# Recording every operation of an attention and mixture-of-experts kernel and issuing it in the order of a list schedule

## The chip, the core and the metric

The kernel runs on one core of a Trainium2 chip. The core has TensorE (PE, matrix products into PSUM; PEld is its weight load), VectorE (DVE), ScalarE (ACT), GpSimd (POOL) and SyncE (SP, which here issues the DMAs). Each engine works through its own queue in the order in which the program was written out, and an instruction at the head of a queue waits for semaphores of other engines. The metric is the device time of one launch in microseconds; lower is better.

## The reference

Linear attention, then a mixture of eight experts with a Sinkhorn-normalised gate, then a gated feed-forward layer, on 2304 tokens of 512 features:

```python
q_s = softmax(q, axis=-1); k_s = softmax(k, axis=2)          # 4 x 8 heads, 576 x 64
kv = einsum('bhsd,bhse->bhde', k_s, v)
x = einsum('bhsd,bhde->bhse', q_s, kv)                       # -> (2304, 512)
P = exp(x @ w_gate - max)                                    # then 8 rounds of
                                                             # row and column normalisation
for e in range(8):                                           # w1: 512 x 1024, w2: 1024 x 512
    out += P[:, e:e+1] * (maximum(x @ w1[e], 0) @ w2[e])
h = out @ w_in                                               # 512 x 2048
return (h * clip(h + 3, 0, 6) / 6) @ w_out                   # 2048 x 512
```

## The kernel before

Every float32 operand of a large product is split into a float16 head and a float16 rest (`split`, lines 230 to 232, and the `hi`/`lo` pairs), and three or four float16 products stand for one float32 product. Products are further formed as seven block products instead of eight, which needs sums of blocks before and after.

The 16 halves of the experts and the 4 quarters of the feed-forward layer are 20 slices, s = 0 to 19. For each slice the tokens pass in three pairs of 384-token groups, p = 0, 1, 2; one (s, p) is a step. In a step TensorE makes the up products of (s, p) while it makes the down products of the step before. Slices 3 to 13 are the FAST stage, 33 steps of `fast_step`, where the down products use seven block products too: the list `line` in that function writes out by hand the order of the units `u0` to `u6` (up) and the parts of `three(t)` (down, one token tile of 128 at a time, three tiles in a step). All seven PSUM banks of that stage have fixed roles (`place`): X, Y, Z for the up products, N0, N1, T and G for the down products. A tile's down products go through bank G in a chain: ScalarE copies N into G (line 1318), TensorE adds products, ScalarE copies one half of G to the other (line 1325), TensorE adds again, and VectorE adds the finished bank onto `acc` (`onto`, line 1310). Only then may the next tile's line 1318 write G.

Beside this run queues of small steps: `ticks`, `side` (the weights of the next slice: load into the one buffer `raw`, absolute maximum, line 261, sums on GpSimd, line 297, and splits, lines 231 and 232) and `back` (conversion of the float64 feed-forward weights, lines 349 to 380). `tick()` takes one or a few of these steps after each unit. So VectorE, ScalarE, GpSimd and SyncE get their instructions in the order in which the hand-written line, the queues and the calls of `tick` interleave; in two middle stretches the framework's own scheduler orders them. In a FAST step VectorE also makes the sums S1 to S4 (`s_sums`, lines 970 to 976) and once a slice T1 to T4.

SBUF tiles for results of the up products come from pools with 16 (`h`) and 5 (`r`) buffers; PSUM tiles come from pools that are closed and opened again at the borders of the FAST stage.

At the start `attention(0)` handles the first two of four batches, then its products feed slice 0, while `attention(1)` (the second two batches) is put beside slices 0 and 1.

## Time and profile before

| what | value |
|---|---|
| median of 2 runs | 1988.99 us (1985.55 to 1992.42) |
| the profiled execution | 1992.86 us, span 1991.1 us |
| granted TensorE clock over the span | 0.977 of full speed |
| TensorE busy | 1843.3 us (93%) |
| VectorE busy | 1423.8 us (72%) |
| ScalarE, GpSimd busy | 990.0 us, 621.2 us |

The span runs from the first to the last instruction of the core. A clock of 1.00 is 2.4 GHz and 0.50 is 1.2 GHz; a mean between them says what part of the stretch was at either. Busy time of TensorE includes matmuls that ran at the lower clock, so it is more than the time that the same work takes at the full one.

### The profile page before, as it was taken

The page shows a single profiled execution, that of the slowest core. Times are in us where ns is not written, and L with a number is a line of the kernel's source. Part 1 is how long each engine was busy: PE and PEld are TensorE (multiplying, and loading weights), DVE is VectorE, ACT ScalarE, POOL GpSimd, SP SyncE. Part 2 cuts the span into 40 slices and gives each one's busy share as a digit, 9 for nine tenths or more (in the row PEclk, how much of TensorE's full clock was granted, in tenths as well). Part 3 has the DMA queues.
Part 4 walks back from the last instruction along what each step waited for, and adds up shares of the span by engine and source line. Part 5 has one row for each costly group of instructions (what it writes and reads, how often), then busy time and mean ns, then how long its engine had stood idle before and what let it go on. Part 6 is the DMA issues. An engine that isn't in the chain of part 4 may idle for free.

```text
span 1991.1 us, 31140 instructions
## 1 busy us (share of the span) xinstructions
PE 1843.3 (93%) x12183; PEld 1135.5 (57%) x12183; DVE 1423.8 (72%) x2438; ACT 990.0 (50%) x2047; POOL 621.2 (31%) x581
## 2 busy tenths in 40 slices
PE   5989999898989898989898989898989999999999
PEld 3455555465666565656566656575745555455554
DVE  8882866778787888787788777857544777687554
ACT  4646454454545455555445555454533556554342
POOL 3323243333332333333333333222222333233111
PEclk8989999999999999999899999999999999999999
DMA  6700022312131212221212222202020000110001
GB/s 206 217 6 1 22 91 103 120 55 93 54 109 54 93 54 93 69 83 64 93 54 93 69 80 74 97 9 91 1 98 1 22 22 1 43 43 22 1 22 74
DMA packets 62611, 129.29 MB, mean 65 GB/s; under 512 B 13952, under 2 KB 18048, under 8 KB 61952
## 3 DMA queue, kind: packets, MB, share of 16 engines
q1 hardware_dynamic: 62464, 127.30, 18.9%
q8 instruction: 95, 1.56, 0.3%
q14 instruction: 52, 0.43, 0.1%
HBM read 105.92 MB, written 18.61 MB: 63 GB/s over the span
## 4 chain that ended last, share of the span: by engine, by line
PE 59%; DVE 24%; ACT 9%; issue 4%; DMA 2%; POOL 1%; SPq 0%; DVEq 0%; POOLq 0%; ACTq 0%
PE y L1118 15%; PE xplace L1173 8%; PE gplace L1289 4%; PE X L1016 4%; PE yplace L1173 4%; DVE w1buf L232 3%; PE gplace L1297 3%; DVE acc L1310 3%; PE tplace L1297 3%; PE tplace L1289 3%; PE Y L1016 2%; ACT w1buf L231 2%; PE B L1016 2%; PE zplace L1173 2%; PE C L1016 2%
## 5 line engine op out<-in xcount | busy, mean ns | idle before, releaser
L1118 PE MATMUL y<-w2buf,h 128*128 128x512 f16 x1944 | 447.8, 379 | 0.5 <-POOL h L1048 0.4
L1191 POOL TENSOR_TENSOR h<-r,h 128x384 f16<-128x384 f32 x198 | 188.9, 954 | 673.7 <-ACT h L1182 637.2
L1173 PEld LDWEIGHTS <-w1buf 128*128 128x128 f16 x2772 | 275.5, 99 | 170.5 <-issue 26.9
L1016 PEld LDWEIGHTS <-w1buf 128*128 128x128 f16 x2268 | 220.4, 98 | 175.0 <-issue 21.0
L1173 PE MATMUL xplace<-xbuf,w1buf 128*128 128x384 f16 x1584 | 308.3, 332 | 6.5 <-ACT r L1194 2.0
L1118 PEld LDWEIGHTS <-h 128*128 128x128 f16 x1944 | 189.1, 98 | 211.1 <-issue 3.3
L1289 PEld LDWEIGHTS <-xbuf 128*128 128x128 f16 x1584 | 155.8, 99 | 152.1 <-issue 77.6
L1048 POOL TENSOR_TENSOR h<-r,h 128x384 f16<-128x384 f32 x90 | 87.3, 970 | 286.7 <-ACT h L1047 255.9
L1173 PE MATMUL yplace<-xbuf,w1buf 128*128 128x384 f16 x792 | 157.4, 337 | 1.3 <-DVE r L1197 1.1
L1182 ACT ACTIVATE h<-r 128x384 f16<-128x384 f32 x264 | 138.0, 523 | 30.4 <-DVE r L1197 24.1
L1194 ACT ACTIVATE r<-xplace 128x384 f32<-128x384 f32 x198 | 96.4, 487 | 106.3 <-PE xplace L1173 103.8
L1043 POOL TENSOR_TENSOR h<-g,h 128x384 f16<-128x384 f32 x72 | 66.8, 928 | 251.5 <-ACT h L1042 220.2
L1016 PE MATMUL X<-xbuf,w1buf 128*128 128x384 f16 x720 | 139.6, 327 | 3.5 <-ACT r L1029 2.7
L1297 PEld LDWEIGHTS <-h 128*128 128x128 f16 x1188 | 118.2, 99 | 36.6 <-issue 0.3
L1289 PEld LDWEIGHTS <-h 128*128 128x128 f16 x1188 | 117.6, 100 | 29.0 <-issue 2.5
L1197 DVE SCALAR_TENSOR_TENSOR r<-yplace,r 128x384 f32<-128x384 f32 x132 | 73.2, 554 | 80.5 <-ACT r L1194 52.7
L1297 PE MATMUL tplace<-w2buf,h 128*128 128x256 f16 x792 | 122.3, 278 | 0.0
L1029 ACT ACTIVATE r<-X 128x384 f32<-128x384 f32 x120 | 58.2, 487 | 126.1 <-PE X L1016 125.8
L1310 DVE SCALAR_TENSOR_TENSOR acc<-gplace,cf,acc 128x512 f32<-128x512 f32 x99 | 74.0, 748 | 45.2 <-PE gplace L1297 42.1
L1289 PE MATMUL gplace<-kvs,xbuf 128*128 128x256 f16 x396 | 62.5, 276 | 44.1 <-ACT gplace L1318 28.3
L1297 PE MATMUL gplace<-w2buf,h 128*128 128x512 f16 x396 | 102.0, 380 | 0.0
L1042 ACT CAST h<-g 128x384 f16<-128x384 f32 x96 | 48.9, 511 | 94.4 <-DVE g L1041 94.4
(670 smaller groups left out, 3308.1 us busy)
## 6 DMA issues: line engine op xcount, KB each, us to landing
raw<-in_moe_w_dram SPq DMA_DIRECT2D x31, 1024.0 KB, 6.0
xbuf<-xkeep SPq DMA_DIRECT2D x77, 384.0 KB, 6.9
scr<-in_moe_w_in_dram SPq DMA_DIRECT2D x16, 512.0 KB, 4.4
scr<-in_moe_w_out_dram SPq DMA_DIRECT2D x16, 512.0 KB, 3.6
xkeep<-xbuf SPq DMA_DIRECT2D x2, 2688.0 KB, 11.0
out_dram<-acc SPq DMA_DIRECT2D x18, 256.0 KB, 2.0
win<-scr SPq DMA_DIRECT2D x16, 256.0 KB, 2.6
wout<-scr SPq DMA_DIRECT2D x16, 256.0 KB, 2.1
```

The lines of the kernel that those rows point to most:

```text
L1016: nc.tensor.matmul(bank[b], w[:, i, wi, c, fs], x[:, i, xi, c, :], start=(first and n == 0), stop=(last and n == 5), skip_group_check=True,)
L1043: eng.tensor_sub(h[:, 1, :], r, h[:, 0, :])
L1048: eng.tensor_sub(h[:, 1, :], c, h[:, 0, :])
L1118: nc.tensor.matmul(ps, hs[grp][fc][:, hi, ts_], w[:, wi, fc, :], start=(n == 0), stop=(n == 11))
L1173: nc.tensor.matmul(o, w[:, i, wi, c, fs], x[:, i, xi, c, :], start=(first and n == 0), stop=(last and n == 5), skip_group_check=True,)
L1182: nc.scalar.activation(h[:, 0, :], c, AF.Relu if relu else AF.Copy)
L1191: nc.gpsimd.tensor_sub(h[:, 1, :], c, h[:, 0, :])
L1194: nc.scalar.activation(r, b, fn, scale=H_DOWN)
L1197: nc.vector.scalar_tensor_tensor(out=r, in0=b, scalar=H_DOWN, in1=r, op0=ALU.mult, op1=ALU.add)
L1289: nc.tensor.matmul(o, a(qf)[:, hl, ts_], b(qf, 1 - hl), start=(first and n == 0), stop=(n == 3), skip_group_check=True,)
L1297: nc.tensor.matmul(o, hs[grp][fc][:, 0, ts_], w[:, 0, fc, cols], start=False, stop=(fc == 3), skip_group_check=True)
L1310: nc.vector.scalar_tensor_tensor(out=a, in0=ps, scalar=factor(s, p, j), in1=a, op0=ALU.mult, op1=ALU.add)
```

## The change

The name `nc` now stands for a `Planner`, which takes down each operation (engine, name, arguments) instead of issuing it. For each it works out a duration (`cost`) and its dependences: by overlap of byte ranges in SBUF and DRAM (`region`, `meet`, `touch`), and by bank in PSUM, where all operations on a bank stay in the order of the code. Matmuls into one place are joined to operations of at most six. `at` is the sum of TensorE's durations up to the place where the operation was taken down.

`order` then makes a list schedule for the five engines. A deadline `late` is passed backwards from the operations that depend on each other, from `at` for TensorE and `at` plus 60 us for the others. Each engine takes, of what can start first (within 30 ns), the operation with the earliest deadline, may leave itself idle for up to 600 ns for one that is more urgent, and starts nothing more than 40 us ahead of `at`. VectorE operations with two wide SBUF operands, or from SBUF to SBUF without a reduction, and all of GpSimd's exclude each other (`lock`). A DMA takes 60 ns of SyncE and lands after 2500 ns plus its bytes over 150 bytes per ns, whatever else is under way. At the end `issue` writes the operations out in that order. `Planner.add` and `issue` replace the framework's scheduling everywhere; the code that takes operations down (`line`, `tick`, the queues) stays as it was, and so do the operations themselves, their shapes and their engines. All rows of the changed program therefore have line 313.

Pools become fixed places: `ring` gives buffers in turn out of one SBUF tile (16 of `h`, 6 of `r`; the feed-forward's `g` tiles get three places of their own), `bank_of` gives one of eight PSUM tiles that exist throughout.

```diff
+class Planner:
...
+    LEAD = 40000.0
+    SLACK = 60000.0
+    HOP = 120.0
+    MARGIN = 300.0
...
+    def cost(self, eng, name, out, ins):
...
+        if eng == "tensor":
+            four = 4 if ins[0].dtype == F32 else 1
+            return 2.0 + n * 0.4167 * four
+        if eng == "scalar":
+            return 170 + 0.8 * n if psum else (720 if n == 512 else 180 + 0.9 * n)
+        big = max([n] + [self.width(x) for x in ins])
+        if eng == "vector":
...
+            if not psum and (half or not two) and name not in ("tensor_reduce", "reduce_max", "reciprocal"):
+                return 150 + big / 1.92
+            return 150 + big / 0.96 + (60 if big >= 512 else 0)
+        if eng == "gpsimd":
+            if big == 512 and len(out.shape) > 2:
+                return 1610
+            return 70 + (2.25 if len(ins) > 1 else 1.2) * big
+        return 2000.0
...
+    def hop(self, a, b):
+        if a["eng"] == b["eng"] and a["eng"] != "sync":
+            return 0.0
+        if a["eng"] == "tensor":
+            return 170.0 + self.HOP
+        if a["eng"] == "sync":
+            return 2500.0 + a["dma"] / 150.0
+        return self.HOP + (self.MARGIN if b["eng"] == "tensor" else 0.0)
+
+    def order(self):
...
+        for o in reversed(ops):
+            late = o["at"] + (0.0 if o["eng"] == "tensor" else self.SLACK)
+            for b in o["post"]:
+                late = min(late, b["late"] - o["dur"] - self.hop(o, b))
+            o["late"] = late
...
+        def pick(e):
+            f = free[e]
+            c = []
+            for o in waits[e]:
+                s = max(f, ready[o["n"]], o["at"] + lag - self.LEAD)
+                if o["lock"]:
+                    s = max(s, lock["gpsimd" if e == "vector" else "vector"])
+                c.append((s, o["late"], o["n"], o))
+            if not c:
+                return None
+            s0 = min(x[0] for x in c)
+            s, d, _, o = min((x for x in c if x[0] <= s0 + 30), key=lambda x: (x[1], x[2]))
+            if e not in ("tensor", "sync"):
+                end = s + o["dur"]
+                for x in sorted((x for x in c if x[0] < end and x[1] < d), key=lambda x: x[1]):
+                    if x[1] + lag < end and d + lag > x[0] + x[3]["dur"] and x[0] - s < 600:
+                        return x[0], x[3]
+            return s, o
...
+            end = s + o["dur"] * (1.0 if e == "tensor" else 1.05)
+            if e == "sync":
+                free[e] = s + 60.0
+                end = s
...
+    def issue(self):
+        for o in self.order():
+            for f, a, k in o["calls"]:
+                f(*a, **k)
...
-    nc = tc.nc
+    real = tc.nc
+    nc = Planner(real)
...
-    pools(u=1, d=2, m=2)
+    pspool = ctx.enter_context(tc.tile_pool(name="ps", bufs=1, space=bass.MemoryType.PSUM))
+    psum = [pspool.tile([P, 512], F32, tag=f"b{i}", name=f"b{i}") for i in range(8)]
+    which = {"A": [0], "B": [1], "C": [2], "D": [3], "d": [4, 5], "m": [6, 7]}
...
+    def ring(tag, shape, dt, bufs):
+        if tag not in rings:
+            rings[tag] = [cpool.tile([P, bufs] + list(shape[1:]), dt, name=f"ring_{tag}"), 0]
+        r = rings[tag]
+        r[1] += 1
+        return r[0][:, (r[1] - 1) % bufs]
...
-        pools(place=1, m=1)
-        for n in ("x", "y", "z", "n0", "n1", "t", "g"):
-            place[n] = banks["place"].tile([P, 512], F32, tag=n, name=f"{n}place")
+        which["m"] = [7]
+        for i, n in enumerate(("x", "y", "z", "n0", "n1", "t", "g")):
+            place[n] = psum[i]
...
+    with tc.manual_schedule():
+        nc.issue()
```

Three places show how rows move. First VectorE's queue before, in slice 8, where the first weights of slice 9 are split (`w1buf` rows, line 232) beside the sums of the up products (lines 972 and 976); `acc` from `gplace` and `tplace` are the rows that set free bank G and bank T.

```order
L1310 SCALAR_TENSOR_TENSOR acc<-n1place,cf_7762,acc 128x512
L972 TENSOR_TENSOR xbuf<-xbuf,h_0_2_8473 128x768
L232 SCALAR_TENSOR_TENSOR w1buf_86<-raw,ws_a__8496,w1buf_86 128x512
L232 SCALAR_TENSOR_TENSOR w1buf_86<-wtmp,ws_a__8496,w1buf_86 128x512
L976 TENSOR_TENSOR xbuf<-h_0_0_8532,xbuf 128x768
L232 SCALAR_TENSOR_TENSOR w1buf_86<-raw,ws_a__8496,w1buf_86 128x512
L1310 SCALAR_TENSOR_TENSOR acc<-gplace,cf_7762,acc 128x512
L1310 SCALAR_TENSOR_TENSOR acc<-tplace,cf_7762,acc 128x512
L232 SCALAR_TENSOR_TENSOR w1buf_86<-raw,ws_a__8496,w1buf_86 128x512
```

The same splits in VectorE's queue of the changed program, one whole token tile (`b6_67` is bank G, `b5_66` bank T, `b3_64` and `b4_65` the N banks, `b1_62` bank Y, `scr_84` the conversion, `xbuf_77` the sums).

```order
L313 SCALAR_TENSOR_TENSOR acc_85<-b6_67,ring_cf_114,acc_85 128x512
L313 SCALAR_TENSOR_TENSOR acc_85<-b5_66,ring_cf_114,acc_85 128x512
L313 TENSOR_TENSOR xbuf_77<-ring_h_105 128x768
L313 TENSOR_TENSOR xbuf_77<-xbuf_77,ring_h_105 128x768
L313 TENSOR_TENSOR xbuf_77<-ring_h_105 128x768
L313 SCALAR_TENSOR_TENSOR w1buf1_79<-raw_82,ring_ws_108,w1buf1_79 128x512 x4
L313 SCALAR_TENSOR_TENSOR acc_85<-b3_64,ring_cf_114,acc_85 128x512
L313 SCALAR_TENSOR_TENSOR scr_84<-scr_84 128x512
L313 TENSOR_TENSOR xbuf_77<-ring_h_105,xbuf_77 128x768
L313 SCALAR_TENSOR_TENSOR ring_r_104<-b1_62,ring_r_104 128x384
L313 SCALAR_TENSOR_TENSOR scr_84<-scr_84 128x512
L313 SCALAR_TENSOR_TENSOR ring_h_105<-ring_r_104,ring_h_105 128x384
```

The four splits that stood on both sides of the `acc` rows of banks G and T now stand behind them, in front of the row of an N bank; two more rows of 128x512 and 128x384 follow in the changed tile before the next row that frees bank G.

SyncE's queue before, from the weights of slice 0 on (`raw` is its first, `acc<-in_moe_w` its second weight, `xbuf<-in_k` and `xbuf<-in_v` the second pair of batches):

```order
L291 DMA raw<-in_moe_w_dram 128x4x512
L1462 DMA wg<-in_moe_w_gate_dram 128x4x8
L458 DMA acc<-in_q_dram 128x192 x14
L327 DMA acc<-in_moe_w_dram 128x4x512
L458 DMA acc<-in_q_dram 128x384 x2
L1588 DMA xkeep_101<-xbuf 128x5376
```

The same place in the changed program:

```order
L313 DMA raw<-in_moe_w_dram 128x4x512
L313 DMA wg<-in_moe_w_gate_dram 128x4x8
L313 DMA xbuf<-in_v_dram 128x9x64 x2
L313 DMA xbuf<-in_k_dram 128x2x576
L313 DMA xbuf<-in_v_dram 128x9x64
L313 DMA xbuf<-in_k_dram 128x2x576
L313 DMA xbuf<-in_v_dram 128x9x64 x3
L313 DMA acc<-in_moe_w_dram 128x4x512
```

Six of the second batches' `v` loads and two of their `k` loads now stand in front of the second weights of slice 0; the fourteen `q` loads that stood there have moved behind.

## Rows read from the trace of the kernel before

**Rows 1.** The page: span, and busy time of TensorE.

```profile
span 1991.1 us, 31140 instructions
PE 1843.3 (93%) x12183; PEld 1135.5 (57%) x12183; DVE 1423.8 (72%) x2438; ACT 990.0 (50%) x2047; POOL 621.2 (31%) x581
```

**Rows 2.** Busy time in five stretches: length, engines, then clock, DMA share, GB/s.

```profile
0.00:54.00 54.00, 31.93 (x449) 20.76 (x449) 44.16 (x78) 26.16 (x44) 18.04 (x24) 0.87 0.57 190
54.00:106.00 52.00, 42.78 (x238) 21.46 (x238) 43.05 (x55) 33.83 (x58) 16.25 (x14) 0.96 0.70 208
106.00:387.60 281.60, 271.08 (x1941) 148.44 (x1940) 182.94 (x367) 135.58 (x267) 105.00 (x105) 0.98 0.15 50
387.60:1449.90 1062.30, 971.37 (x6756) 668.67 (x6755) 809.65 (x1334) 542.99 (x1207) 342.48 (x302) 0.97 0.21 72
1449.90:1937.00 487.10, 475.75 (x2556) 251.46 (x2554) 318.53 (x565) 236.88 (x447) 131.38 (x129) 0.99 0.08 28
```

**Rows 3.** Waits of TensorE from 387.6 to 1449.9 us: total us, times, longest.

```profile
PE gplace L1289 <- ACT gplace L1325: 35.7, 25, 2.0
PE gplace L1289 <- ACT gplace L1318: 28.3, 15, 2.5
PE gplace L1289 <- DVE xbuf L972: 15.7, 9, 2.8
```

**Rows 4.** Timeline of TensorE: start, length, what, idle before it.

```profile
812.79 0.60 PE L1289 MATMUL gplace<-kvs,xbuf 128*128 128x256 f16 x4
...
841.12 0.78 PE L1289 MATMUL gplace<-kvs,xbuf 128*128 128x256 f16 x4
...
855.36 1.03 PE L1297 MATMUL gplace<-w2buf,h 128*128 128x512 f16 x4
...
861.69 0.60 PE L1289 MATMUL gplace<-kvs,xbuf 128*128 128x256 f16 x4 [2.47 <-ACT gplace L1318]
```

**Rows 5.** Timeline of VectorE behind the wait at 861.69 us.

```profile
858.25 1.61 DVE L976 TENSOR_TENSOR xbuf<-h,xbuf 128x768 f16<-128x768 f16 x1
859.79 0.74 DVE L232 SCALAR_TENSOR_TENSOR w1buf<-raw,ws_a__8496,w1buf 128x512 f16<-128x512 f32 x1
860.45 0.74 DVE L1310 SCALAR_TENSOR_TENSOR acc<-gplace,cf,acc 128x512 f32<-128x512 f32 x1
```

**Rows 6.** Groups of 387.6 to 1449.9 us with shapes: busy us, mean ns, idle before.

```profile
L1197 DVE SCALAR_TENSOR_TENSOR r<-yplace,r 128x384 f32<-128x384 f32 x132 | 73.2, 554 | 80.5 <-ACT r L1194 52.7 <-PE yplace L1173 27.6
L970 DVE TENSOR_TENSOR xbuf<-h,h 128x768 f16<-128x768 f16 x64 | 55.9, 874 | 0.0
```

**Rows 7.** One line's instructions there: shortest, median and longest in ns.

```profile
L970 DVE TENSOR_TENSOR xbuf<-h,h x64: 544/553/1626, 407.6 to 1420.5; 128x768 f16<-128x768 f16 x64
```

**Rows 8.** Timeline of SyncE's issues, start and length.

```profile
21.35 8.42 SPq L458 DMA_DIRECT2D acc<-in_q_dram  x14
33.08 0.38 SPq L327 DMA_DIRECT2D acc<-in_moe_w_dram  x1
...
61.20 18.12 SPq L478 DMA_DIRECT2D xbuf<-in_v_dram  x8
```

**Rows 9.** Timeline of VectorE near the start.

```profile
39.07 1.02 DVE L685 TENSOR_TENSOR xbuf<-f,xbuf 128x384 f16<-128x384 f32 x2 [1.30 <-ACT xbuf L684]
...
48.07 2.33 DVE L261 TENSOR_REDUCE am_b__539<-acc 128x1 f32<-128x1024 f32 x2
...
97.34 4.14 DVE L605 TENSOR_TENSOR acc<-acc,qm 128x1536 f32<-128x1536 f32 x2
101.40 2.33 DVE L261 TENSOR_REDUCE am_b__871<-raw 128x1 f32<-128x1024 f32 x2
```

**Rows 10.** Timeline of TensorE behind those reductions.

```profile
105.51 0.29 PE L208 MATMUL cm_b__894<-identb,wm_b__880 128*128 128x128 bf16 x1 [7.10 <-DVE wm_b__880 L269]
```

**Rows 11.** DMA issues of the page: count, KB each, median us to landing.

```profile
xbuf<-xkeep SPq DMA_DIRECT2D x77, 384.0 KB, 6.9
...
acc<-in_moe_w_dram SPq DMA_DIRECT2D x1, 1024.0 KB, 5.4
```

More of the change, by code (lines that the diff above doesn't have):

```diff
@@ L108, in view, with bank_of @@
         return ap.rearrange(f"p ({dims}) -> p {dims}", **{f"x{j}": shape[j] for j in range(1, len(shape))})
-    def col(name, w=1, dt=F32):
-        return sm.tile([P, w], dt, tag=f"c{w}{dt}", name=name, bufs=8)
+    rings = {}
+    def ring(tag, shape, dt, bufs):
[4 more added lines that the diff above has]
+        return r[0][:, (r[1] - 1) % bufs]
+    def col(name, w=1, dt=F32):
+        return ring(f"c{w}" + ("i" if dt == I32 else ""), [P, w], dt, 8)
+    def bank_of(tag, shape):
+        b = which[tag]
+        b.append(b.pop(0))
+        flat = psum[b[-1]]
+        n = 1
+        for d in shape[1:]:
+            n *= d
+        if len(shape) == 2:
+            return flat[:, :n]
+        dims = " ".join(f"x{j}" for j in range(1, len(shape)))
+        return flat[:, :n].rearrange(f"p ({dims}) -> p {dims}", **{f"x{j}": shape[j] for j in range(1, len(shape))})
     def psm(shape, name, dt=F32):
-        return banks["m"].tile(shape, dt, tag="m", name=name)
+        return bank_of("m", shape)
     def rt(name):
-        return rpool.tile([P, GN], F32, tag="r", name=name)
+        return ring("r", [P, GN], F32, 6)
     ident = cpool.tile([P, P], F32, name="ident")
@@ L271, in fin @@
         def fin():
-            st["s"] = sm.tile([P, 2], F32, tag="ws", name=f"ws_{name}", bufs=8)
+            st["s"] = ring("ws", [P, 2], F32, 8)
             pow2(st["mm"], st["s"], top)
@@ L422, in tile_attention_moe_ffn @@
     AW, VW = H * QR * D, H * QR * (D + 1)
-    half = lambda t: t.rearrange("p j d -> p (j d)")
     GA = QR - GJ
@@ L517, in kback @@
             if first:
-                ps = banks["d"].tile([P, len(cs) * P], F32, tag="d", name=f"kb{b0}_{cs[0]}")
+                ps = bank_of("d", [P, len(cs) * P])
             else:
@@ L547, in kv @@
                 t["kv"] = [
-                    banks["u"].tile([P, 512], F32, tag="AB"[i], name=f"kv{b0 + i}")[:, : NKC * (D + 1)]
+                    bank_of("AB"[i], [P, 512])[:, : NKC * (D + 1)]
                     .rearrange("p (c d) -> p c d", d=D + 1)
@@ L596, in qmax @@
             if "qm" not in t:
-                t["qm"] = sm.tile([P, H, QR], F32, tag="qm", name=f"qm{pr}", bufs=2)
+                t["qm"] = ring("qm", [P, H, QR], F32, 2)
             nc.vector.tensor_reduce(
@@ L916, in factors @@
         r = res[s]
-        ws = sm.tile([P, 1], F32, tag="wsc", name=f"wsc{s}", bufs=3)
+        ws = ring("wsc", [P, 1], F32, 3)
         nc.vector.tensor_mul(ws, r["s1"][:, 1:2], r["s2"][:, 1:2])
@@ L934, in factor @@
         if p not in cf:
-            co = sm.tile([P, 1], F32, tag="co", name=f"co{s}_{p}", bufs=3)
+            co = ring("co", [P, 1], F32, 3)
             nc.vector.tensor_scalar(
@@ L1008, in up_burst @@
             tags = {"X": "AD"[bursts[0] % 2], "Y": "B", "Z": "C"}
-        bank = {b: banks["u"].tile([P, 512], F32, tag=g, name=f"{b}{nm}")[:, :GN] for b, g in tags.items()}
+        bank = {b: bank_of(g, [P, 512])[:, :GN] for b, g in tags.items()}
         fs = slice(qf * P, (qf + 1) * P)
@@ L1112, in down_tile @@
         j = g * GJ + t
-        ps = banks["d"].tile([P, DM], F32, tag="d", name=f"y{s}_{j}")
+        ps = bank_of("d", [P, DM])
         ts_ = slice(t * P, (t + 1) * P)
@@ L1179, in hi @@
         def hi(c, grp, fc, relu):
-            h = hpool.tile([P, 2, GN], F16, tag="h", name=f"h{grp}{s}_{p}_{fc}", bufs=HB)
+            h = ring("h", [P, 2, GN], F16, HB)
             hs[grp][fc] = h
@@ L1441, in x2_steps @@
         return steps
-    with tc.manual_schedule():
-        make_identity(nc, ident)
+    if True:
+        make_identity(real, ident)
         nc.vector.memset(ones, 1.0)
@@ L1511, in bank @@
             if qd == QB22:
-                return banks["u"].tile([P, 512], F32, tag="AB"[i], name=name)[:, :GN]
+                return bank_of("AB"[i], [P, 512])[:, :GN]
             count[0] += 1
             if (count[0] - 1) % 4 < 2:
-                return banks["u"].tile([P, 512], F32, tag="CD"[i], name=name)[:, :GN]
-            return banks["d"].tile([P, DM], F32, tag="d", name=name)[:, :GN]
+                return bank_of("CD"[i], [P, 512])[:, :GN]
+            return bank_of("d", [P, DM])[:, :GN]
         f = t0["forms"](0, bank)
@@ L1652, in tile_attention_moe_ffn @@
     first, last = order.index((FAST[0], turns[FAST[0]][1])), order.index((FAST[-1] + 1, 0))
-    with tc.manual_schedule():
+    if True:
         for sp in order[FROM:first]:
@@ L1664, in tile_attention_moe_ffn @@
             unit(lambda: None)
-        pools(u=1, d=2, m=2)
+        which["m"] = [6, 7]
         for sp in order[last + 1 : TO]:
@@ L1669, in tile_attention_moe_ffn @@
         prev = step(*sp, prev)
-    with tc.manual_schedule():
+    if True:
         for sp in order[AGAIN:]:
```

223 lines of the change are left out of this document (202 added, 21 removed).

## The prediction

> **What bounds the kernel now.** I read the page first. TensorE is busy for 1843.3 us of 1991.1, so at first sight 148 us are to be had [rows 1]. Then I cut the span into stretches, since a mean share over stages with different limits says little [rows 2]. Each stretch gives two losses of TensorE: its length less its busy time, and the clock below 1.00. The start (0 to 106 us) loses 31 us of idle time; the stretch to 387.6 us loses 10.5; the FAST stage, 387.6 to 1449.9 us, loses 91; the stretch behind it 11.4. The FAST stage also runs at a mean clock of 0.97.
>
> What the FAST stage could take is read from a clean step. From one tile's first product into bank G at 812.79 us to the same place one step later, at 841.12 us, is 28.3 us, and in between TensorE hardly pauses [rows 4]. The stage has 33 such steps: 935 us. It takes 1062.3 us. So 127 us lie above its own clean pace, 91 of them idle and the rest work at 1.2 GHz behind the pauses. This is the stage on which the forecast rests.
>
> Who ends TensorE's pauses there: the copy by ScalarE from one half of bank G to the other (35.7 us) and its copy from N into G (28.3 us), then VectorE's sums (15.7 us) [rows 3]. But ScalarE is not the cause. At 861.69 us TensorE had waited 2.47 us for line 1318; the down products into G had been issued from 855.36 us with a length of 1.03 us, so `acc` could have been taken from G at about 856.4 us [rows 4]. VectorE took it at 860.45 us, some 4 us late. In front of it in the queue stood a sum of 1.61 us and weight splits of 0.74 us each, none of them urgent [rows 5]. The queue order of VectorE is what TensorE waits for.
>
> The sum of 1.61 us is itself a wait: the line it is like (970) has a median of 553 ns, a shortest of 544 and a longest of 1626 [rows 7]; 64 of them have a mean of 874 ns [rows 6]. So each lost some 0.3 us on the mean.
>
> **The change, part by part.** All sums are made against the profiled execution, 1992.86 us, which is 3.9 us above the median of the two runs.
>
> (1) The FAST stage. No operation is added or taken away; VectorE, ScalarE and GpSimd get another order, and TensorE small shifts. The diff's order shows the kind of move: before, three splits and a sum stood between an N row and the rows that free G and T; now four splits stand behind those rows, in front of an N row, and an N bank has a twin. Cover for such a tile: TensorE has 28.3 / 3 = 9.4 us of work in it. VectorE's rows in the changed tile are nine of 128x512 at 0.74 us [rows 5], four sums at 0.553 us [rows 7], three of 128x384 at 0.554 us [rows 6] and one short one on the conversion, put at 0.55 us: 6.7 + 2.2 + 1.7 + 0.55 = 11.1 us. So VectorE is 1.6 us over in that tile, and the pauses won't all go. I count such an overrun once for each of the two weights of 11 slices: 22 times 1.6 us, 35 us that stay. Over the whole stage there is room: VectorE's 809.65 us [rows 2] stand against 935 us.
> The bounds: if all overruns are worked off in the neighbouring tiles, 127 us go; if half of the loss stays, 64. I take 127 - 35 = 92 us, because the tile's own rows give the 35.
>
> (2) The middle (106 to 387.6) and the late stretch (1449.9 to 1937) lose 10.5 and 11.4 us of idle time. There is no clean step to compare with; between nothing and 22 us I take half, 11 us.
>
> (3) The start. One part gains. At 105.51 us TensorE had waited 7.1 us for the scale of slice 1's second weights [rows 10]; its absolute maximum ran on VectorE at 101.40 us, behind 4.14 us of subtractions and other work for the second pair of batches [rows 9]. In the changed order this maximum stands ahead of those. If it goes, 7 us are won; what is late next is the split of the same weights, which is needed either way.
> One part may lose. The second weights of slice 0 were issued at 33.08 us, behind fourteen loads of `q` (8.42 us of queue) [rows 8]; they land 5.4 us later [rows 11], at 38.5 us, and VectorE looked at them only at 48.07 us [rows 9]. Now six loads of `v` and two of `k` stand ahead of them. Eight such `v` loads took 18.12 us of queue [rows 8]; six take 13.6 us, and the two of `k` (576 KB each, put at the same pace per KB) some 9 us. They can't start before the first products have freed their places, which is the work of the first 20 to 27 us, so the weights are issued somewhere between 33 and 46 us and land between 38.5 and 51 us. In VectorE's queue the maximum of these weights stands ahead of most rows that make slice 0's inputs, the first of which ran at 39.07 us [rows 9]. The price is therefore between 0 and 12 us, all of it on the path, since TensorE has nothing else yet. I take 2 us, near the lower end, because the issue at 33.08 us was itself behind a wait for the places of `q` that doesn't change, and because the early loads take later waits away. Net for the start: -5 us, with ends at -7 (all of the gain) and +12 (all of the price, and no gain).
> The Trainium skill, page "DMA: Bandwidth & Descriptors", section "Issuing engines are not separate DMA queues", says that all DMAs of a core run on the same 16 engines and interleave. The planner prices each DMA as if it were alone, at which price part (3) would cost nothing; by the page's rule it costs up to the whole 12 us. The trace sides with the page: with 0.70 of the DMA engines busy the core moved 208 GB/s [rows 2].
>
> (4) Fixed rings and banks. They give the same number of `h` buffers, one more of `r`, the same banks. I cost them at nothing: the dependences by place that the pools gave are the same ones by bytes. If a bank were shared where it was not before, one tile would wait for another, which is rival C.
>
> Sum: 1992.9 - 92 - 11 - 5 = 1885 us; less the 3.9 us by which the profiled execution stands above the median, 1881 us.
>
> **The rivals.**
> A, the forecast: pauses of the FAST stage fall to a third, 1880 us.
> B, VectorE becomes the bound: its 809.65 us in the stage hold some of the waiting that [rows 6, 7] show, but little of it goes, the fixed order drifts against the real times, and overruns add up; half of the 127 us stays. 1992.9 - 64 - 5 - 3.9 = 1920 us. For it: 11.1 us of rows in a tile of 9.4. Against: whole steps at 28.3 us exist already.
> C, the change doesn't do what it says: the list is made with prices that don't hold, queues stand behind other rows than before, and what is won at one bank is lost at another. 1985 us, give or take 20. Against: the prices agree with rows here, for instance 150 + 384 / 0.96 = 550 ns against a mean of 554, and 150 + 512 / 0.96 + 60 = 743 ns against 740 [rows 5, 6].
> D, slower: DMAs come late in every slice. Each slice of the FAST stage reloads a set of tokens from `xkeep` in seven DMAs of 384 KB, 77 in all [rows 11]. The planner has each land after 2.5 + 2.6 = 5.1 us; sharing 208 GB/s [rows 2], the seven take 12.9 us, and one weight load that slips between them adds 1024 KB or 5 us: 13 us late. Eleven times that is 143 us of TensorE's time, and 1880 + 143 = 2023 us before the clock, some 2040 with it. It decides from (1989 - 1880) / 11 = 10 us a slice on. Against: the same DMAs stand a whole step (28.3 us) ahead of their use, the planner may start them up to 40 us ahead, and no wait for them is among TensorE's [rows 3].
> By the section of the Trainium skill's page "DMA: Bandwidth & Descriptors" named above, D would be the outcome if the loads had no lead; the trace bears the shared rate out, not the lateness.
>
> **How the numbers follow.** A 0.62, B 0.20, C 0.11, D 0.07. The forecast is A, 1880 us. Its own ends: all parts at their best, 1992.9 - 127 - 22 - 7 - 3.9 = 1833 us; FAST at half with the start at its worst, 1992.9 - 64 + 12 - 3.9 = 1937 us. The range leaves out C and D and the outer edge of A's best case: 1840 to 1937 us. Two per cent of 1989 us is 40 us, about what a measurement of this kernel can tell from no change. Faster by more than that (under 1949 us) are A and B, 0.82; within it most of C, 0.10; slower D and a little of C, 0.08.
>
> **What would show it.** In the changed profile: the FAST stage takes 960 to 980 us at a clock of 0.99 or 1.00 (right), or over 1000 (B). The waits of TensorE for the copies into G fall from 64 us to under 25. The rows of `acc` from bank G start within a microsecond of the products' end. The mean of the sums comes down towards 553 ns if GpSimd and VectorE are really kept apart. The wait of 7.1 us near 105 us is gone; a new wait between 39 and 51 us shows part (3)'s price. D would show as TensorE waiting for a DMA into `xbuf` once a slice. The forecast is wrong if TensorE's pauses keep their sum and only change their names, or if the start grows by more than 12 us.

## The result and the profile after

| what | before | after |
|---|---|---|
| median of 2 runs each | 1988.99 us | 1841.88 us (1840.94 to 1842.81) |
| ratio, 95% interval | | 0.926, 0.919 to 0.933 |
| the profiled execution, its span | 1992.86, 1991.1 us | 1842.81, 1841.0 us |
| granted TensorE clock over the span | 0.977 | 0.989 |

The changed kernel is 147 us faster, and 38 us faster than the forecast of 1880 us. It lies 1.9 us above the lower end of the range, 1840 us. The page of the changed kernel, against [rows 1]:

```profile
span 1841.0 us, 30821 instructions
...
PE 1794.4 (97%) x12183; PEld 1128.1 (61%) x12183; DVE 1374.5 (75%) x2438; ACT 984.3 (53%) x2047; POOL 600.6 (33%) x581
```

Of the 150 us by which the span shrank, TensorE's busy time gives 49 and its idle time 101. The same stretches as in [rows 2], cut where the same operations stand now (FAST begins at 384.62 us and ends at 1317.38 us); the columns are as there:

```profile
0.00:54.00 54.00, 27.05 (x375) 18.03 (x376) 36.18 (x57) 18.86 (x28) 18.51 (x23) 0.79 0.81 251
54.00:106.00 52.00, 46.63 (x535) 27.05 (x536) 48.07 (x73) 34.89 (x62) 15.29 (x12) 0.93 0.31 91
106.00:384.62 278.62, 271.73 (x1713) 147.36 (x1712) 179.13 (x375) 140.49 (x279) 103.45 (x107) 0.99 0.21 70
384.62:1317.38 932.76, 929.44 (x6763) 660.53 (x6762) 781.25 (x1334) 540.84 (x1208) 324.68 (x303) 1.00 0.25 81
1317.38:1787.00 469.62, 469.62 (x2553) 250.67 (x2551) 307.18 (x564) 236.76 (x449) 131.00 (x129) 1.00 0.08 26
```

The FAST stage went from 1062.3 to 932.8 us (-129.5): 33 steps of 28.27 us, the clean pace that [rows 4] showed for one step. Up to its beginning 3.0 us were won, behind it (1449.9 to 1991.1 us before, 1317.38 to 1841.0 us now) 17.6. These make -150.1.

What is left of [rows 3] in the FAST stage (TensorE's waits: total us, times, longest):

```profile
PE b L313 <- ACT b L313: 1.5, 2, 0.9
PE b L313 <- DVE acc L313: 0.9, 1, 0.9
```

The place that the prediction read in [rows 4, 5] looks like this now, first in TensorE's timeline, then in VectorE's:

```profile
789.73 1.03 PE L313 MATMUL b<-w2buf,ring_h 128*128 128x512 f16 x4
```

```profile
790.79 0.75 DVE L313 SCALAR_TENSOR_TENSOR acc<-b,ring_cf,acc 128x512 f32<-128x512 f32 x1 [0.74 <-PE b L313]
791.46 1.11 DVE L313 TENSOR_TENSOR xbuf<-ring_h 128x768 f16<-128x768 f16 x1
```

The last products into the bank end at 789.73 + 1.03 = 790.76 us, and VectorE takes `acc` 0.03 us later, in place of some 4 us. VectorE now waits for TensorE (0.74 us), and the sum that is in no hurry stands behind the row that frees the bank. The sums themselves, against [rows 6, 7] (groups with mean ns, then one group's shortest, median and longest):

```profile
L313 DVE TENSOR_TENSOR xbuf<-ring_h 128x768 f16<-128x768 f16 x130 | 90.5, 696 | 0.3 <-POOL ring_h L313 0.3
...
L313 DVE TENSOR_TENSOR xbuf<-ring_h,xbuf 128x768 f16<-128x768 f16 x65 | 37.1, 571 | 1.2 <-POOL ring_h L313 1.2
```

```profile
L313 DVE TENSOR_TENSOR xbuf<-ring_h x128: 542/551/1626, 398.1 to 1290.6; 128x768 f16<-128x768 f16 x128
```

The median is 551 ns, but the longest is still 1626 ns and the largest group's mean 696. Of the 256 sums in this stretch 37 take more than 0.7 us (62 before), and beside every one of them the timelines have an instruction of GpSimd: the planner's exclusion of VectorE and GpSimd holds in part.

The start, in the timelines of TensorE, VectorE and SyncE:

```profile
50.46 3.53 PE L313 MATMUL b<-ring_h,xbuf 64*64 64x192 f32 x40 [1.65 <-DVE xbuf L313]
...
114.42 0.87 PE L313 MATMUL b<-ident,xbuf 128*128 128x128 f32 x3 [6.20 <-DVE kvs L313]
```

```profile
52.98 1.21 DVE L313 TENSOR_REDUCE ring_c<-acc 128x1 f32<-128x1024 f32 x1
54.11 1.01 DVE L313 TENSOR_TENSOR xbuf<-b,xbuf 128x384 f16<-128x384 f32 x2
```

```profile
28.68 6.90 SPq L313 DMA_DIRECT2D xbuf<-in_v_dram  x3
37.17 0.37 SPq L313 DMA_DIRECT2D acc<-in_moe_w_dram  x1
```

Slice 0's second weights are issued at 37.17 us in place of 33.08 [rows 8], and the first row that makes slice 0's inputs runs at 54.11 us in place of 39.07 [rows 9]: 15 us late, which is made up by the beginning of FAST. The wait of 7.1 us of [rows 10] is gone, but one of 6.2 us for another VectorE result (`kvs`) now ends at 114.42 us.

### The profile page after: what moved, and what is told of

Its sections match the earlier page's. It is cut to its first block, busy times and chain, and to the rows that moved or that the text cites. A ratio compares the mean times of both kernels' runs of the same rounds, so it can differ in the third digit from the quotient of the medians.

```text
span 1841.0 us, 30821 instructions
## 1 busy us (share of the span) xinstructions
PE 1794.4 (97%) x12183; PEld 1128.1 (61%) x12183; DVE 1374.5 (75%) x2438; ACT 984.3 (53%) x2047; POOL 600.6 (33%) x581
## 5 line engine op out<-in xcount | busy, mean ns | idle before, releaser
L313 PE MATMUL b<-xbuf,w1buf 128*128 128x384 f16 x5040 | 895.5, 327 | 0.6
L313 PE MATMUL b<-w2buf,ring_h 128*128 128x512 f16 (+1 forms) x3924 | 767.5, 336 | 1.1 <-DVE acc L313 0.9
L313 PEld LDWEIGHTS <-ring_h 128*128 128x128 f16 x4320 | 421.7, 98 | 276.7 <-issue 4.2
L313 POOL TENSOR_TENSOR ring_h<-ring_r,ring_h 128x384 f16<-128x384 f32 x288 | 274.4, 954 | 806.7 <-ACT ring_h L313 773.7
L313 ACT ACTIVATE ring_r<-b 128x384 f32<-128x384 f32 x432 | 211.6, 490 | 360.7 <-PE b L313 359.0
L313 DVE SCALAR_TENSOR_TENSOR acc<-b,ring_cf,acc 128x512 f32<-128x512 f32 x351 | 261.2, 748 | 151.4 <-PE b L313 134.8
L313 DVE SCALAR_TENSOR_TENSOR ring_r<-b,ring_r 128x384 f32<-128x384 f32 x342 | 189.4, 554 | 169.9 <-PE b L313 134.5
L313 ACT COPY b<-b 128x256 f32<-128x256 f32 (+1 forms) x462 | 168.6, 374 | 217.5 <-PE b L313 119.6
L313 ACT ACTIVATE ring_h<-ring_r 128x384 f16<-128x384 f32 x294 | 153.3, 522 | 35.7 <-DVE ring_r L313 30.9
L313 POOL TENSOR_TENSOR scr<-scr 128x512 f32<-128x512 f32 x64 | 85.1, 1330 | 23.9 <-ACT scr L313 21.7
L313 DVE TENSOR_REDUCE ring_c<-raw 128x1 f32<-128x1024 f32 x78 | 92.4, 1207 | 0.0
L313 DVE SCALAR_TENSOR_TENSOR ring_h<-ring_r,ring_h 128x384 f16<-128x384 f32 x96 | 60.4, 629 | 11.0 <-ACT ring_h L313 10.5
```

What stands on the lines that cost most here:

```text
L313: f(*a, **k)
```

## The experiments

The FAST stretch is measured alike in all, from the first to the last of the 198 products of one tile (`lg`) that only this stage has; in the kernel before and after these are (start of the first and of the last at the end):

```profile
L1289 PE MATMUL gplace<-lg,h x198: 269/273/421, 399.2 to 1447.9; 128*128 128x256 f16 x198
```

```profile
L313 PE MATMUL b<-lg,ring_h x198: 272/273/273, 394.2 to 1315.4; 128*128 128x256 f16 x198
```

So 1048.7 us before and 921.2 after, 127.5 us less. "Idle" and "busy" are TensorE's in that stretch. An engine in code order gets its operations in the order in which the code took them down; a free one goes by the list schedule.

| kernel | in code order | total us | ratio to before (95%) | FAST us | idle | busy |
|---|---|---|---|---|---|---|
| before | as issued | 1988.99 | 1 | 1048.7 | 90.8 | 957.9 |
| e1 | all five | 2061.43 | 1.038 (1.035 to 1.041) | 1048.9 | 93.2 | 955.7 |
| e2 | all but VectorE | 2075.96 | 1.045 (1.042 to 1.048) | 1047.4 | 89.3 | 958.1 |
| e5 | all but ScalarE | 2029.27 | 1.020 (1.017 to 1.023) | 1010.2 | 70.0 | 940.2 |
| e6 | TensorE, GpSimd, SyncE | 2025.65 | 1.018 (1.015 to 1.021) | 1044.4 | 96.6 | 947.8 |
| e3 | TensorE | 1870.99 | 0.942 (0.939 to 0.945) | 929.6 | 8.0 | 921.6 |
| e4 | VectorE | 1905.52 | 0.959 (0.956 to 0.962) | 953.2 | 26.1 | 927.2 |
| e7 | ScalarE | 1936.98 | 0.973 (0.970 to 0.976) | 975.9 | 38.9 | 937.0 |
| e9 | GpSimd | 1918.38 | 0.965 (0.963 to 0.966) | 978.5 | 42.2 | 936.3 |
| e10 | SyncE | 1923.94 | 0.967 (0.966 to 0.969) | 988.0 | 48.7 | 939.3 |
| after | none | 1841.88 | 0.926 (0.919 to 0.933) | 921.2 | 3.3 | 917.9 |
| e8 | none, no exclusion | 1842.59 | 0.926 (0.923 to 0.929) | 917.6 | 0.7 | 916.9 |
| e11 | none, DMA prices | 1839.69 | 0.925 (0.924 to 0.927) | 920.5 | 2.5 | 918.0 |
| e12 | TensorE's first operations | 1838.81 | 0.925 (0.923 to 0.927) | 921.1 | 3.2 | 917.9 |

The theories have numbers in the expectations: theory 1 is the prediction's (VectorE's queue order), theory 2 TensorE's own order, theory 3 the rings and banks; theory 4 is that VectorE's and ScalarE's queues hold each other up, theory 5 that ScalarE's order is the cause by itself, theory 6 that SyncE's or GpSimd's order holds up the rest.

**e1_code_order.** Rings, banks and the recorded operations stay, but all are issued in the order of the code (by the number under which an operation was taken down, behind what it depends on); the list schedule isn't used.

```diff
+    def code_order(self):
+        left = {o["n"]: len(o["pre"]) for o in self.ops}
+        heap = [o["n"] for o in self.ops if not left[o["n"]]]
...
+            o = self.ops[heapq.heappop(heap)]
...
     def order(self):
...
+        return self.code_order()
```

> The changed kernel (planner's dependences, rings, banks), but every operation is issued in the order in which the code took it down; no list schedule. Theory 1 (the order of VectorE's queue makes the gain) and theory 2 (TensorE's own new order makes it): 1985 us, 1960 to 2010, with waits of TensorE for the copies into bank G of some 60 us again. Theory 3 (the fixed rings and banks, and the absence of the framework's own scheduling and pool waits, make it): under 1870 us.

Measured: FAST 1048.9 us, as before to 0.2 us, with 63.9 us of waits for the copies, as theories 1 and 2 said; but 72 us more in total, above the 1960 to 2010 us that they gave. So the rings and banks alone give nothing in the FAST stage, and neither does the taking down. The changed kernel differs from this one in the order only, so the gain there is the order's; whether the same order would give it with the pools of before wasn't tried. What this kernel loses outside FAST it loses against the kernel before, whose two middle stretches the framework's scheduler ordered; that this is the reason wasn't tried apart.

**e2_vector_only.** VectorE by the list schedule, the other four engines in code order: an engine in `KEEP` may start an operation only when it is the next of its own code order.

```diff
+    KEEP = ('tensor', 'scalar', 'gpsimd', 'sync')
...
+        queue = {e: deque(o["n"] for o in self.code_order() if o["eng"] == e) for e in self.KEEP}
...
             for o in waits[e]:
+                if e in queue and o["n"] != queue[e][0]:
+                    continue
...
+            if e in queue:
+                queue[e].popleft()
```

> The list schedule may reorder VectorE alone; TensorE, ScalarE, GpSimd and SyncE keep the order of the code. Theory 1: most of the gain is there, under 1890 us. Theory 2: over 1950 us. Theory 3: like the changed kernel, under 1870 us, but then e1_code_order is too.

Measured: FAST 1047.4 us, 1.3 us of the 127.5. Theory 1, which gave most of the gain to this run, falls. TensorE's waits there, against [rows 3]:

```profile
PE b L336 <- ACT b L336: 67.6, 34, 6.4
PE b L336 <- ACT ring_r L336: 14.0, 32, 4.5
```

The copies between banks keep their 64 us (67.6), though VectorE is free to release the bank early.

**e3_all_but_tensor.** Only TensorE in code order.

```diff
+    KEEP = ('tensor',)
```

> The list schedule with TensorE held to the order of the code, the other four engines free. Theory 1: 1845 to 1865 us, the FAST stage at 935 to 945 us. Theory 2: over 1930 us.

Measured: FAST 929.6 us; TensorE's own order is worth 8.4 us there, and 17 us before it (the stretch begins at 411.4 us in place of 394.2). Theory 2 falls for the FAST stage. The total of 1870.99 us lies a little above the 1845 to 1865 us of theory 1, because of the loss ahead of FAST.

**e4_all_but_vector.** Only VectorE in code order.

```diff
+    KEEP = ('vector',)
```

> The list schedule with VectorE held to the order of the code, the other four free. Theory 1: over 1940 us, since urgent rows of VectorE again stand behind splits and sums. Theory 2: under 1880 us, since TensorE fills its pauses with other products.

Measured: FAST 953.2 us, and a total between what theories 1 and 2 said. With VectorE's order as it was, 95.5 of the 127.5 us are still won: its order costs 32 us where all others are free, and gives 1.3 where all others are held.

**e5_scalar_only.** Only ScalarE by the list schedule.

```diff
+    KEEP = ('tensor', 'vector', 'gpsimd', 'sync')
```

> The list schedule may reorder ScalarE alone; the other four keep the order of the code. Measured from the first to the last product with T4's second half in the FAST stage (1048.7 us before, 921.2 changed, 1048.9 in code order, 1047.4 with VectorE alone free). Theory 4 (VectorE's and ScalarE's queues hold each other up, so freeing one does nothing): 1030 to 1050 us there, 2050 to 2080 us in all. Theory 5 (ScalarE's order is the cause by itself): under 960 us there, under 1960 in all. Theory 6 (GpSimd's and SyncE's order, the weights' sums and loads): 1030 to 1050.

Measured: FAST 1010.2 us, 38.5 us of the gain, which neither theory 4 (1030 or more) nor theory 5 (under 960) gave. The waits change their names:

```profile
PE b L336 <- DVE xbuf L336: 25.3, 12, 4.5
PE b L336 <- DVE ring_r L336: 17.6, 14, 2.6
PE b L336 <- ACT b L336: 15.3, 19, 1.8
```

The copies fall from 64 to 15.3 us, and VectorE's results, in their old order, end 43 us of waits.

**e6_scalar_vector.** ScalarE and VectorE by the list schedule, the others in code order.

```diff
+    KEEP = ('tensor', 'gpsimd', 'sync')
```

> The list schedule may reorder ScalarE and VectorE; TensorE, GpSimd and SyncE keep the order of the code. The same stretch of the FAST stage. Theory 4: under 960 us. Theory 5: under 960 us. Theory 6: over 1020 us. In all it stays above the changed kernel, since loads and GpSimd near the start keep the code's order: 1890 to 1960 by theories 4 and 5.

Measured: FAST 1044.4 us, 34 us worse than ScalarE alone, as only theory 6 said (the total is 3.6 us better).

```profile
PE b L336 <- DVE ring_c L336: 31.6, 13, 5.2
PE b L336 <- ACT ring_r L336: 30.0, 33, 12.0
PE b L336 <- DVE xbuf L336: 18.3, 10, 10.6
```

```profile
L336 POOL TENSOR_TENSOR scr<-scr 128x512 f32<-128x512 f32 x60 | 80.9, 1348 | 163.9 <-ACT scr L336 148.4 <-DVE scr L336 8.2 <-DVE ring_wsc L336 4.9
```

The copies into G are down to 6.7 us, but single waits are now as long as 12 us. GpSimd, in code order, stands 148.4 us at the weight conversion (`scr`) for ScalarE, whose part of the conversion is not urgent to the list schedule; behind it in GpSimd's queue are operations that TensorE does need (8.7 us of waits for `ring_h` from GpSimd). In the changed kernel this group waits 21.7 us for ScalarE. So a free queue beside a held one can be no gain: the free one may put off what the held one has at its head. That this alone makes the 1044 us wasn't tried apart.

**e7_all_but_scalar.** Only ScalarE in code order.

```diff
+    KEEP = ('scalar',)
```

> The list schedule with ScalarE held to the order of the code, the other four free. The same stretch. Theory 4: as with VectorE held (953 us), 945 to 990. Theory 5: over 1020 us. Theory 6: under 945 us.

Measured: FAST 975.9 us: ScalarE's order costs 55 us, TensorE's waits being 23.6 us for copies and 14.6 for `ring_r`, both ScalarE's. That is in theory 4's range (945 to 990); theory 5 (over 1020) falls.

**e8_no_lock.** The exclusion of VectorE and GpSimd left out of the schedule.

```diff
-        op["lock"] = (
...
+        op["lock"] = False
```

> The planner without the mutual exclusion of VectorE and GpSimd (no operation is marked as locking), all else as changed. If the exclusion matters: 1860 us or more, FAST stretch over 930 us, sums (128x768) at a mean of 680 ns or more. If not: within 6 us of the changed kernel, since VectorE has room to wait.

Measured: 1842.59 us, FAST 917.6 us: no change. The sums take a little longer than in the changed kernel (719 against 696 ns, 675 against 571):

```profile
L308 DVE TENSOR_TENSOR xbuf<-ring_h 128x768 f16<-128x768 f16 x128 | 92.1, 719 | 0.9 <-POOL ring_h L308 0.9
...
L308 DVE TENSOR_TENSOR xbuf<-ring_h,xbuf 128x768 f16<-128x768 f16 x64 | 43.2, 675 | 7.2 <-POOL ring_h L308 7.2
```

The Trainium skill, page "SBUF — State Buffer", section "🔬 SBUF: two separate sides", says that a GpSimd operation that reads SBUF and a VectorE operation with two SBUF inputs lock each other out for a whole instruction. The traces agree: all 37 sums of over 0.7 us in the changed kernel's stretch, and all 54 here, stand beside a GpSimd instruction, while of the 218 of at most 0.6 us in the changed kernel 16 do. But the time isn't lost to the kernel: with 17 more long sums FAST took 3.6 us less, and the total was the same.

**e9_all_but_gpsimd and e10_all_but_sync.** Only GpSimd, or only SyncE, in code order.

```diff
+    KEEP = ('gpsimd',)
```

```diff
+    KEEP = ('sync',)
```

> GpSimd takes its operations in the recorded code order, the other four engines by the list schedule. Theory 6 (with TensorE, GpSimd and SyncE held the FAST stretch was 1044 us, with TensorE alone held 930, so that GpSimd or SyncE is what undid the freeing of ScalarE and VectorE): GpSimd's half of it says that the weight sums and conversions in code order hold VectorE's splits and with them the products, a FAST stretch of 980 to 1045 us and some 1910 to 2000 in all. If SyncE's loads are the cause instead, this run stays near 921 to 935 us in FAST and 1845 to 1865 in all. If no single engine is the cause but any held queue costs its part (VectorE 32, ScalarE 55 us), it lies between, 940 to 980.

> SyncE issues its DMAs in the recorded code order, the other four engines by the list schedule. If the loads are what undid the freeing of ScalarE and VectorE: FAST stretch 980 to 1045 us. If it was GpSimd: 921 to 935 in FAST. At the start the loads of keys, values and queries stand in code order again; if the late values behind the queries were the price there, the first form products start near 40 us in place of 50 and FAST starts up to 8 us earlier than with all five free; with FAST at 925 that makes 1835 to 1850 in all.

Measured: FAST 978.5 and 988.0 us. Neither half of theory 6 is alone right: each of the two queues, held, costs 57 and 67 us. With SyncE held the start didn't gain either: the first form products came at 47.64 us, not near 40, and the stretch began at 405.2 us, 11 us later than with all five free. SyncE's own longest waits, first with SyncE held, then in the changed kernel:

```profile
SPq L336 <- POOL scr L336: 719.2, 30, 47.2
```

```profile
SPq L313 <- ACT scr L313: 330.6, 27, 26.3
...
SPq L313 <- POOL scr L313: 79.3, 26, 11.8
```

In code order SyncE stands 719 us in total, up to 47 us at a time, at stores of converted weights that wait for GpSimd, and the loads behind wait with them, as in these rows of its timeline, where nothing is issued for 15 us ahead of the store `win` and a load of tokens (`xkeep`) follows it:

```profile
629.54 0.37 SPq L336 DMA_DIRECT2D scr<-in_moe_w_in_dram  x1
645.42 0.32 SPq L336 DMA_DIRECT2D win<-scr  x1
...
646.87 0.45 SPq L336 DMA_DIRECT2D xbuf<-xkeep  x1
```

But the length of SyncE's waits doesn't make the difference: all of them together are some 910 us here and 850 in the changed kernel, where ScalarE and VectorE end most of them, and in the kernel before SyncE stood 593 us at the same stores without a wait of TensorE for a load. What differs, as far as the rows show, is what stands behind. With SyncE held TensorE waits for tokens that are not loaded, which it does in the FAST stretch of no other kernel of the table:

```profile
PE b L336 <- DMA xbuf<-xkeep: 13.8, 8, 3.8
```

That is 13.8 of the 48.7 us of idle time; how SyncE's order makes the rest wasn't traced.

Outside FAST the same runs give another picture. From the stretch's end to the end of the span the kernel before takes 543.2 us and the changed one 525.6; with TensorE, GpSimd or SyncE held it is 525.5 to 527.9, with VectorE held 536.0 and with ScalarE held 549.5. So in this late part a held queue costs time only where it is VectorE's or ScalarE's.

**e11_dma_model.** All five engines by the list schedule, with DMAs that queue on one wire and take SyncE 480 ns each.

```diff
...
-                free[e] = s + 60.0
-                end = s
+                free[e] = s + 480.0
+                wire = max(wire, s) + o["dma"] / 240.0
+                end = wire + 1600.0 - self.hop(o, None)
```

> The schedule of all five engines as in the changed kernel, but with DMAs priced as the trace shows them: 480 ns of SyncE for each issue in place of 60, and a shared wire of 240 bytes per ns behind which each transfer queues, landing 1600 ns later, in place of 2500 ns plus its bytes over 150 per ns whatever else is under way. If the planner's blindness to that is what cost the start, TensorE's operations there stand in the order in which their data lands and the first form products come 5 to 10 us earlier: 1830 to 1838 in all, FAST as it was (918 to 925). If the start is set by the deadlines (queries before values) and not by the price, no change: 1838 to 1846.

Measured: 1839.69 us, no change that can be told from 1841.88. The first form products start at 49.88 us (50.46 in the changed kernel). What fills the time ahead of them is in TensorE's timeline:

```profile
30.68 0.90 PE L315 MATMUL b<-ident,ring_r 128*128 128x128 f32 x3 [7.50 <-POOL ring_r L315]
31.50 0.93 PE L315 MATMUL b<-xbuf 64*64 64x65 f32 x22
32.36 0.47 PE L315 MATMUL b<-ident,ring_r 128*128 128x128 f32 x1
32.76 0.47 PE L315 MATMUL b<-xbuf 64*64 64x65 f32 x2
33.17 0.69 PE L315 MATMUL b<-ident,ring_r 128*128 128x128 f32 x2
33.78 0.48 PE L315 MATMUL b<-xbuf 64*64 64x65 f32 x4
...
49.88 3.52 PE L315 MATMUL b<-ring_h,xbuf 64*64 64x192 f32 x40 [1.71 <-DVE xbuf L315]
```

Transposes of the queries and products of keys and values take turns. The planner counts 110 ns for each of the latter (2 + 65 x 0.4167 x 4), while 22 of them take 0.86 us; that this price makes the turns is argued, not tried. Read the starts: a group of 2 products holds TensorE for 0.41 us, a single transpose for 0.40, a further one for 0.21.

**e12_first_products.** As e11, and TensorE's operations below number 300 (up to the first form products) in code order: products first, then transposes.

```diff
+        first = deque(o["n"] for o in ops if o["eng"] == "tensor" and o["n"] < 300)
...
+                if e == "tensor" and first and o["n"] != first[0]:
+                    continue
```

> The schedule with the DMA prices of the run before, and TensorE's first operations (those taken down up to the first form products, numbers below 300) in code order: first all products of keys and values, then the transposes of the queries. In the trace of the run before TensorE made 24 such transposes and 98 key-value products in turn, one to four at a time, without idle time, from 30.7 to 45.8 us = 15.1 us; in the kernel before 88 such products in a block took 2.7 us and the 24 transposes in a block 6.1 us, 8.8 us together. If it is the turns between the two shapes that cost, the first form products start some 6 us earlier (43 to 45 us in place of 49.9) and the whole takes 1831 to 1836 us. If the values land so late that the products wait for them, or something behind the form products sets the start, the time stays at 1838 to 1842; if TensorE, which now waits at each product in turn, loses more, 1842 to 1850.

Measured: 1838.81 us (1838.60 to 1839.23; e11 had 1838.81 to 1840.64). The turns are gone:

```profile
30.10 2.23 PE L320 MATMUL b<-xbuf 64*64 64x65 f32 x72 [5.15 <-issue]
32.26 3.07 PE L320 MATMUL b<-ident,ring_r 128*128 128x128 f32 x12
35.86 3.27 PE L320 MATMUL b<-ident,ring_r 128*128 128x128 f32 x12 [0.53 <-ACT ring_h L320]
...
41.49 2.44 PE L320 MATMUL b<-ring_h,xbuf 64*64 64x192 f32 x40 [1.57 <-ACT xbuf L320]
...
106.43 0.29 PE L320 MATMUL b<-identb,ring_c 128*128 128x128 bf16 x1 [5.66 <-DVE ring_c L320]
```

The form products start 8.4 us earlier, as the first outcome says (and 2 us more), but the whole gains 0.9 us, as the second outcome says. The FAST stretch begins 2.8 us earlier (390.3 against 393.1). TensorE now waits 5.7 us for VectorE at 106.43 us, and VectorE is busy for this share of 54 to 106 us:

```profile
54.00:106.00 52.00, 41.57 (x505) 24.69 (x504) 49.92 (x78) 33.52 (x57) 15.44 (x13) 0.98 0.16 50
```

49.92 of 52 us. So behind the first form products VectorE's work sets the pace of the start; this is read from the rows, no run with less VectorE work there was made. Both lie 2 to 3 us (0.1 to 0.2%) under the changed kernel, which its interval can't tell from no change.

## Why the prediction was right, and where its steps were not

**What bounds the kernel: right in place, wrong in cause.** The FAST stage was where the time was, and its clean pace was what it came down to. The step "The queue order of VectorE is what TensorE waits for", with "ScalarE is not the cause", failed. VectorE's order alone gave 1.3 us (e2); with it left as it was 95.5 us were won all the same (e4); ScalarE's alone gave 38.5 (e5). In the FAST stage each held queue costs its part while the other four go by the list schedule: TensorE's 8, VectorE's 32, ScalarE's 55, GpSimd's 57, SyncE's 67 us. That is 219 us where 127.5 are to be had, so these are not shares of the loss before; part of them may come from a held queue beside four that were ordered anew. And freeing VectorE, ScalarE or both gives 1, 38 or 4 us (the other three were not freed alone), so the gains don't add up either. What is shown is that the order of the queues together makes the gain, and that neither VectorE's nor ScalarE's does alone. What fits it is a chain through several queues, each with something at its head that waits for another, as GpSimd's does in e6 and SyncE's in e10; which link costs what stays open. The row `acc` at 860.45 us [rows 5] was one link of it.

**Part (1), sized -92, measured -129.5.** The step that failed is "35 us that stay": 22 tiles with VectorE 1.6 us over its time. They left nothing: 33 steps at 28.27 us. That VectorE has more rows than time in one tile doesn't count when the planner may start its rows up to 40 us ahead; over the stage it has 781 us of work in 933, and what counts is that no tile's urgent rows stand behind the rest. The prediction's own other end, 127, was the right term. Of the 127.5 us of the narrower stretch 87.5 are TensorE's idle time and 40.0 its busy time (957.9 to 917.9): products at the lower clock behind waits; the longest of the 198 was 421 ns and is now 273.

**Part (2), sized -11, measured at some -21.** The middle's idle time fell by 3.6 us (see part 3). The late stretch gave 17.5 us in place of half of 11.4: TensorE is busy there for all of 469.62 us. The step that failed is that the prediction counted its idle time alone; the stretch behind FAST also had a clock of 0.99 [rows 2], now 1.00, so busy time fell as well, from 475.75 to 469.62 us.

**Part (3), sized -5, with ends at -7 and +12.** Up to FAST 3.0 us were won, the middle's part of (2) among them: from 106 us to FAST idle time fell by 3.6 us (10.5 to 6.9), up to 106 us it grew by 1.0 (31.3 to 32.3). So the start came out at about nothing. The step that failed is the gain: the wait of 7.1 us is gone as named, but one of 6.2 us stands 9 us later. The price was not paid at the second weights, whose issue moved by 4 us, within the window that the prediction gave; TensorE's waits from 54 to 63 us are for the first inputs (`xbuf`). These came 13 us later (37.16 to 50.46 us for the form products), of which 8.4 went with TensorE's turns between transposes and products (e12) and 0.6 with the price of the DMAs (e11); the rest is unexplained. Without the turns only 2.8 of the 8.4 us were left at the beginning of FAST. The prediction took from the Trainium skill's page "DMA: Bandwidth & Descriptors", section "Issuing engines are not separate DMA queues", that all DMAs of a core run on the same engines, and worked out that the planner's price for a DMA as if it were alone may cost up to 12 us. With a shared price (e11) the time stayed; and the 208 GB/s that it read as the shared rate were no ceiling, since the changed start moved 251.

**Part (4), nothing: right in FAST** (e1: 0.2 us). Outside it no run separates the rings and banks from the order.

**What was luck.** The range's far end is built on the clean step, which is the same whichever queue makes the pauses; so the time could lie in the range though the cause was wrong. It held by 1.9 us: the FAST stage and the late stretch gave 38 and 12 us more than their terms, and the start none of its 5. Had the start gained the 7 us that the prediction hoped for, the time would have been below the range.

**Rivals.** B (half of the loss stays) fell to the reason given against it: whole steps at the clean pace existed. C is what single queues do: e2 and e5 move TensorE's waits to other names, with 1 and 38 us of gain. D didn't come: there is no wait for a DMA in FAST. Its mechanism exists, though: with SyncE in code order TensorE waits 13.8 us for `xkeep` loads (e10).

**What would show it.** The FAST stage is at clock 1.00 as said, but at 932.8 us it is shorter than the 960 to 980 given for A. The copies at 1.5 us in place of 64 and `acc` within 1 us (in the tile shown) are as said. The mean of the sums didn't come down to 553 ns, only their median did, and it was of no consequence (e8).

## What to carry to other kernels

A wait's releaser is the last link of a chain. Where several in-order queues feed each other, ask of each queue what stands at its head and for whom; an experiment that frees one queue may give nothing although the whole gives all, so hold one and free the rest as well. To size such a change, take the clean step, count the rows of each engine against it over a stage and not over a tile, and add to the idle time what the clock costs behind it. A list schedule need not have every price right: without the exclusion (e8) and with other DMA prices (e11) the time was the same. Look for an odd interleaving where TensorE looks busy, as the one beside the price of 110 ns for products of 39; here undoing it gave 0.9 us.

## What the runs showed of the hardware

Waits cost more than their length. In the kernel before, TensorE waited 2.47 us at 861.69 us [rows 4] and 1.97 us at 865.73 us. Six products that had taken 1.14 us ahead of these waits took 2.13 us behind them:

```profile
858.08 1.14 PE L1173 MATMUL xplace<-xbuf,w1buf 128*128 128x384 f16 x6
...
867.43 2.13 PE L1173 MATMUL yplace<-xbuf,w1buf 128*128 128x384 f16 x6
```

The granted clock was 1.00 (2.4 GHz) from 858.08 to 859.20 us and 0.50 (1.2 GHz) from 867.4 to 869.5 us. Over the kernels of the table, idle time of TensorE in FAST goes with longer busy time for the same products: 26 us idle with 9 more busy than the changed kernel (e4), 42 with 18 (e9), 49 with 21 (e10), 91 with 40 (before). That is 0.3 to 0.5 us of slower products for each us waited, in these runs.

Turns between products of 64 rows and transposes of 128 cost TensorE time that counts as busy. In e11 the turns ran from 30.68 to 45.14 us, 14.5 us for 21 transposes and 98 products (the expectation of e12 counted 24 and 15.1 us; the last three transposes came behind, at 45.80 us). In e12 24 transposes and 72 products, in blocks, are 8.6 us of the timeline; at their pace 21 and 98 would take 8.6 us as well, an estimate from 2.23 us for the 72 products and 6.34 for the 24 transposes. Both ran at the lower clock, 1.2 GHz (windows of e11, then e12):

```profile
30.70:44.70 14.00, 14.00 (x119) 8.66 (x120) 3.55 (x7) 2.88 (x6) 9.21 (x10) 0.50 0.53 153
```

```profile
30.10:39.20 9.10, 8.57 (x97) 6.47 (x98) 7.25 (x13) 4.87 (x9) 7.82 (x8) 0.50 0.96 235
```

The Trainium skill, page "TensorEngine Tiling (Array Packing)", section "Key Properties", says that a change of the tiling mode drains TensorE; the trace agrees, with 0.40 us for a single transpose between products and 0.21 for a further one behind it.
